# DeltaNet and a quick-GELU feed-forward on one core: the chunk inverses built from blocks of 8, with the joins on TensorE

## The chip, the core and the metric

The kernel runs on one core of a Trainium2 chip. The metric is device time in microseconds of one execution of the whole program. Engines are TensorE (PE, with its weight loads PEld), VectorE (DVE), ScalarE (ACT), GpSimd (POOL) and SyncE (SP, which mostly issues DMA transfers).

## What is computed

A delta-rule attention over 4 batches, 8 heads, 768 steps and head size 48 is followed by a feed-forward of 3072 tokens, 384 to 2048 to 384.

```python
k_n = k / (np.linalg.norm(k, axis=-1, keepdims=True) + 1e-06)
for t in range(S):
    y[:, :, t] = np.einsum('bhd,bhde->bhe', q[:, :, t], state)
    v_old = np.einsum('bhde,bhd->bhe', state, kt)
    state = state + bt[:, :, :, None] * np.einsum('bhd,bhe->bhde', kt, vt - v_old)
...
h = x @ w_in
g = h * (1.0 / (1.0 + np.exp(-1.702 * h)))
return (g @ w_out).astype(np.float32)
```

The weights come in 8-byte floats and are converted on the chip to 4-byte ones.

## The kernel before

The sequence is cut into 6 chunks of C = 128 steps. A unit is a chunk of one batch with all 8 heads (units 0 to 3, first chunk), or, from the second chunk on, half a chunk of 64 steps of two batches (class `Half`). Within a chunk the recurrence becomes a triangular system: with the Gram matrix of the normalized keys (`gram`), the corrected values U solve a unit lower triangular system. Its diagonal blocks of BS = 32 are inverted ahead of time, and the solve runs block by block.

**Inverses.** `diagonal(n)` computes the 32x32 diagonal Gram blocks of a first-chunk unit on TensorE (tile `psD`); VectorE scales them by beta into `XBs`. `invert(c)` puts the 128 blocks of all units on the 128 partitions (VectorE transposes, tiles `NT` and `YB`). For i = 1 to 15 it forms row i of the inverse of both 16-blocks of each 32-block at once: a product into tile `P` and a sum over it (line 308 on). For the first chunk (c = 0) it stops there, scales by beta and transposes back to `XBs`. For later chunks it joins the two 16-blocks to 32 on VectorE as well (lines 318 to 341, ten products and ten sums), scales by beta and sends the result through DRAM to `XBs`. Its input there comes from the Gram matrices through DRAM: `send_blocks` writes blocks to `Nd`, `load_diagonals` reads them into `NT`, and `bL` holds the betas, fetched by 16 transfers issued on POOL.

**The first join.** `merge(pair, ...)` (line 734) joins the 16-blocks of two first-chunk units to 32 on TensorE: VectorE transposes the blocks, a burst of 32x32-tile matmuls forms `psP`, ScalarE evicts it masked by `upper`, a second burst adds into `psZ`, ScalarE copies the corner into `XBs`.

**Solving the first chunk.** Units go in pairs, (0, 1) and (2, 3). `hops` lists eight steps for a pair: `solve` of one 32-block of a unit (`psU`, ScalarE copy into U) beside `below` of the other unit, which subtracts the solved block from the rows under it (accumulated in `psV`, which `gather` has filled with the values; ScalarE copies the next block). `put_out` then forms the outputs `psY` and the state. ScalarE copies them to `xT`, `last` and `ST`, and six transfers move `last` into its place in `xT` (three issued on SP, three on POOL). The scores `psQ` are copied to `M` and masked on POOL (`select`).

**Filling.** `fill(us)` emits pieces of VectorE's background work until their estimated costs reach `us`. The background (line 370) is, in order: conversion of all of w_in and of the first 8 row groups of w_out, then `invert(1)`, then conversion of the other 8 row groups. One conversion piece has five VectorE operations and one on ScalarE (a clamp). `feed()` emits one step (three matmuls of 256 columns) of `hidden`, the first feed-forward product (tile `ph`). `warm(n)` emits n matmuls on constants whose results are not used (tile `ps_warm`). `paced` makes a weight fetch wait for a certain result by a one-element POOL copy.

**Order.** Nearly every operation is issued through wrappers (line 139) that keep an engine's instructions in the order of the program text, so traces show line 139 for them, and so do DMAs issued through `sync` (SP) and `other_queue` (POOL). A few POOL operations, such as the differences of w_out formed in `combined` (shown as line 1118), are placed by the compiler's scheduler.

After the second pair's hops the program emits 25 rounds of `fill(1.0)` and `feed()` together with norms, transposes and Grams of the third chunk's units, the scores of unit 4, half of `both_written` (second feed-forward product, tile `po`), `fill(9.5)`, and from then on slots (`slot(n, share)`). A slot solves a block of unit n and one of unit n + 1, writes outputs, and fills TensorE with feed-forward work from a queue. The inverse of unit 4 is first read at the beginning of slot 3.

## Time and profile before

| what | us |
|---|---|
| median of 3 runs | 692.75 |
| the runs | 686.65, 693.12, 692.75 |
| the profiled execution | 683.09 |
| its span, first to last instruction | 681.4 |
| TensorE busy in the span | 660.4 (97%) |
| VectorE busy | 479.5 (70%) |
| ScalarE busy | 233.6 (34%) |
| GpSimd busy | 269.4 (40%) |
| mean granted clock of TensorE | 0.991 |

The profile is of one execution. A busy TensorE is not TensorE at its peak, since the ends of its matmuls are modelled. A program row such as "TENSOR_TENSOR P<-NT,YB 128x8" names the written tile, the read tiles and partitions x elements. A logical matmul of 4-byte floats has two records, so three matmuls of `hidden` show as x6. A bracket at the end of a row gives the idle time of the engine before it and what ended it.

### The profile page before, as it was taken

What the parts mean: (1) busy time and instruction counts of PE and PEld (TensorE: products, weight loads), DVE (VectorE), ACT (ScalarE), POOL (GpSimd) and SP (SyncE); (2) the same over time, 40 slices, a digit from 0 to 9 for tenths busy, and PEclk for the clock granted to TensorE, in tenths of its full rate; (3) what the DMA queues carried; (4) which work ended last, traced back from release to release, by engine and by line L of the source; (5) the groups of instructions that cost most, each with busy time, mean ns of one, the idle gap of its engine ahead of it and who ended that gap; (6) DMA issues with size and microseconds to landing.
All of it is one profiled execution on the core that took longest, in us unless ns stands there. A gap on an engine that the chain in (4) does not pass through costs nothing.

```text
span 681.4 us, 21731 instructions
## 1 busy us (share of the span) xinstructions
PE 660.4 (97%) x9290; PEld 563.4 (83%) x9290; DVE 479.5 (70%) x890; ACT 233.6 (34%) x571; POOL 269.4 (40%) x282
## 2 busy tenths in 40 slices
PE   9899899799999999999999999999999999999997
PEld 4766678566678998998998988988988988989997
DVE  4889799983788997996997996997976970200000
ACT  2558463632333233333333233233233233322120
POOL 4032844320286634635535526426305205105041
PEclk9799999989999999999999999999999999999999
DMA  9567575263334435335335244244231130100101
GB/s 174 105 165 175 128 218 99 44 155 81 83 74 92 96 63 109 79 67 104 71 67 116 67 90 88 66 86 79 62 78 19 38 75 2 30 2 6 26 0 24
DMA packets 149632, 54.61 MB, mean 80 GB/s; under 512 B 137824, under 2 KB 142656, under 8 KB 149536
## 3 DMA queue, kind: packets, MB, share of 16 engines
q1 hardware_dynamic: 146368, 46.62, 32.7%
q0 software_dynamic: 3168, 6.61, 3.7%
q8 instruction: 73, 1.20, 0.8%
q14 instruction: 23, 0.19, 0.1%
HBM read 38.37 MB, written 13.63 MB: 76 GB/s over the span
## 4 chain that ended last, share of the span: by engine, by line
PE 86%; DVE 6%; ACT 2%; DMA 2%; issue 2%; SPq 1%; DVEq 0%; ACTq 0%
PE po L139 34%; PE ph L139 32%; PE four L139 7%; PE psU L139 3%; PE psR L139 2%; PE psG L139 2%; DVE P L139 2%; DVE w_out L139 2%; PE ps_warm L139 1%; DVE YB L139 1%; DMA TW<-in_q_dram 1%; PE psQ L139 1%; SPq L139 1%; PE psV L139 1%; DVE NT L139 1%
## 5 line engine op out<-in xcount | busy, mean ns | idle before, releaser
L139 PE MATMUL ph<-xT,w_in 128*128 128x256 f32 x1152 | 261.0, 384 | 2.3 <-ACT gT L139 2.0
L139 PEld LDWEIGHTS ph<-xT,w_in 128*128 128x128 f32 x1152 | 215.9, 190 | 33.8 <-ACT gT L139 2.4
L1118 POOL TENSOR_TENSOR gT<-gT 128x512 f32<-128x512 f32 x80 | 103.0, 1298 | 97.9 <-ACT gT L139 66.0
L139 PE MATMUL po<-w_out,gT 128*128 128x192 f32 (+1 forms) x720 | 138.4, 347 | 0.0
L139 DVE TENSOR_TENSOR P<-NT,YB 64x8 f32<-64x8 f32 (+13 forms) x195 | 124.8, 640 | 5.8
L139 PEld LDWEIGHTS po<-w_out,gT 128*128 128x128 f32 x720 | 118.5, 190 | 11.0 <-ACT o L139 0.5
L139 ACT ACTIVATE gT<-ph 128x512 f32<-128x512 f32 x90 | 53.8, 598 | 154.8 <-PE ph L139 154.8
L139 DVE TENSOR_REDUCE YB<-P 64x4 f32<-64x8 f32 (+13 forms) x195 | 78.4, 402 | 6.7
L139 PE MATMUL po<-TW,gT 128*128 128x192 f32 x480 | 81.8, 328 | 0.0
L139 PEld LDWEIGHTS po<-TW,gT 128*128 128x128 f32 x480 | 78.1, 190 | 0.7
L984 POOL TENSOR_SCALAR_AFFINE_SELECT M<-M 64x512 f32<-64x512 f32 x40 | 29.1, 727 | 90.0 <-ACT M L139 88.8
L139 DVE TENSOR_TENSOR o<-o,late 128x192 f32<-128x192 f32 x20 | 6.6, 356 | 68.1 <-ACT late L139 67.9
L139 ACT COPY VU<-psU 32x384 f32<-32x384 f32 x96 | 45.2, 470 | 21.3 <-PE psU L139 14.9
L139 DVE TENSOR_TENSOR VU<-VU,psR 32x384 f32<-32x384 f32 x40 | 22.1, 553 | 36.6 <-PE psR L139 35.9
L400 POOL TENSOR_TENSOR rn<-ssq,half 128x8 f32<-128x8 f32 x12 | 22.3, 1858 | 52.6 <-DVE ssq L139 52.6
L139 DVE TENSOR_TENSOR VU<-VU,four 128x384 f32<-128x384 f32 x19 | 10.4, 548 | 46.1 <-ACT M L139 46.0
L109 POOL DMA_DIRECT2D KN<-in_k_dram x24 | 17.2, 716 | 58.4 <-PE four L139 56.7
L139 ACT COPY o<-po 128x192 f32<-128x192 f32 (+1 forms) x44 | 14.7, 334 | 74.6 <-PE po L139 72.5
L139 PEld LDWEIGHTS psU<-VU,XBs 32*32 32x32 f32 x1536 | 27.4, 105 | 13.5 <-issue 8.5
L139 PE MATMUL psU<-VU,XBs 32*32 32x48 f32 x1536 | 32.6, 203 | 0.3 <-ACT VU L139 0.2
L139 DVE TENSOR_TENSOR P<-NT 64x512 f32<-64x512 f32 (+7 forms) x45 | 30.5, 679 | 1.1
L139 DVE TENSOR_REDUCE NT<-P 64x32 f32<-64x512 f32 (+9 forms) x45 | 30.0, 668 | 1.5
(167 smaller groups left out, 752.1 us busy)
## 6 DMA issues: line engine op xcount, KB each, us to landing
VU<-in_v_dram SPq DMA_DIRECT2D x40, 96.0 KB, 2.8
out_dram<-o SPq DMA_DIRECT2D x40, 96.0 KB, 2.2
QW<-in_q_dram SPq DMA_DIRECT2D x76, 48.0 KB, 2.2
Kd<-KN SPq DMA_DIRECT2D x56, 64.0 KB, 2.2
late<-Kd SPq DMA_DIRECT2D x14, 256.0 KB, 2.8
KN<-in_k_dram POOLq DMA_DIRECT2D x30, 96.0 KB, 3.1
w_out<-in_moe_w_out_dram SPq DMA_DIRECT2D x7, 384.0 KB, 3.8
NT<-Nd SPq DMA_DIRECT2D x20, 128.0 KB, 2.7
```

The lines of the kernel that those rows point to most:

```text
L109: dma(out=place(dst, n)[rows, :, 0:D], in_=src[b, :, t, :].rearrange("h p d -> p h d"),)
L139: return lambda *a, **kw: tc.keep_in_program_order(op(*a, **kw))
L400: nc.gpsimd.tensor_tensor(rn, ssq, half, op=ALU.pow)
L984: nc.gpsimd.affine_select(out=M, in_=M, compare_op=ALU.is_gt, fill=0.0, base=0, pattern=[[0, H], [1, CH]], channel_multiplier=-1,)
L1118: (engine or nc.gpsimd).tensor_tensor(o, a, b, op=op)
```

## The change

The diff is cut here; "..." marks what is left out.

The first chunk. `diagonal` scales by a beta that is zero outside each row's own eighth and sums over eighths, so `XBs` holds only the 8x8 diagonal blocks. `invert_first` takes the place of `invert(0)`: four 8x8 blocks per partition, seven rounds. `spread` writes the inverses back into block-diagonal 32-blocks. `merge` joins on TensorE in three levels, 8 to 16, 16 to 32 and 32 to 64, for both pairs. In the first pair VectorE does part of the evictions, in the second ScalarE does. `solve` and `below` work on blocks of 64, so a pair has three steps, and a step emits both units.

```diff
+        for hh in range(2):
+            vec.tensor_tensor(
+                split[:, hh], ps[hh].rearrange("p j (g k) -> p j g k", g=NE),
+                bG[:, n * H + hh : (n + 1) * H : 2].broadcast_to([128, NP, NE, E8]), op=ALU.mult,
+            )
+        vec.tensor_reduce(
+            XBs[:, n, :, 0:E8], flat.rearrange("p (h g k) -> p h k g", h=H, g=NE), axis=AX.X, op=ALU.add
+        )
...
+    def invert_first():
...
+        vec.transpose(lanes_N.rearrange("p i k -> p k i"), by_lanes(XBs[:, :, :, 0:E8]))
...
+        for i in range(1, E8):
+            P = wk.tile([128, NE, i, i], F32, tag="P", name="P", bufs=1)
+            tt(
+                P, eighths(lanes_N, i * E8, [[0, i], [1, i]]), eighths(lanes_Y, 0, [[E8, i], [1, i]]),
+                op=ALU.mult,
+            )
+            vec.tensor_reduce(
+                eighths(lanes_Y, i, [[E8, i]]), P, axis=AX.X, op=ALU.add, negate=True
+            )
+        tt(lanes_N, lanes_Y, bI.broadcast_to([128, BS, E8]), op=ALU.mult)
+        vec.transpose(packed.rearrange("p n k -> p k n"), lanes_N.rearrange("p j i -> p i j"))
...
+    def merge(pair, area, banks, first):
...
+        for s in (E8, 2 * E8):
...
+            turn_blocks()
+            for X, o, m in zip(pair, odd, Pm):
+                ps = psum(0, "psP", HS)
+                for h in range(H):
+                    for r in rows:
+                        pe.matmul(
+                            ps[r, h, :], lhsT=X.G[r, h, r], rhs=o[r, h], start=True, stop=True,
+                            skip_group_check=True,
+                        )
...
+            for x, o, t, m in zip(Z, odd, XT, Pm):
+                ps = psum(1, "psZ", HS)
...
+                if first:
+                    vec.tensor_tensor(o, o, split, op=ALU.add)
+                else:
+                    act.copy(o, split)
+                yield
+        turn_blocks()
...
+        for i, X in enumerate(pair):
+            W = wides[X.n] = wide[:, i]
...
+        def solve(self, blk):
+            r = slice(blk * CH, (blk + 1) * CH)
+            psU = bank("psU")
+            for h in range(H):
+                pe.matmul(
+                    psU[r, h, :], lhsT=wides[self.n][r, h, :], rhs=self.V[r, h, :],
+                    start=True, stop=True,
+                )
             act.copy(self.U[r], psU[r])
```

The tiles of `invert_first` and the 64-blocks (`wide`) all lie in `NT`. The order around them is written anew: the Gram matrices come after `invert_first`, most `warm` calls go, and the weights of the later quarters, the values of units 2 and 3 and the first rows of w_out are fetched at other places. The second pair runs inside passes of one `feed()` and `fill(2.2)` each. `load_diagonals` and the 16 transfers of `bL` come after the outputs of unit 3.

```diff
+    for X in pair[:2]:
+        X.solve(0)
+    pair[1].gather()
+    next(scored[2])
+    fill(1.5)
+    for X in pair[:2]:
+        X.below()
+    next(scored[3])
+    fill(1.5)
+    paced(pair[0].US[CH : CH + 1, 0:1], 2, 1)
+    for X in pair[:2]:
+        X.solve(1)
...
     put_out(pair[0])
     fill(2.0)
     put_out(pair[1])
+    scaling = roots_second(areas)
+    next(scaling)
+    merging = merge(pair[2:], area, ((ps_seq, "seq"), (ps_seq, "seq")), False)
+    fetch_in(2, js=(2,))
+    for b in range(HB, B):
+        load_values(b, sync)
+    for j in range(KC):
+        fetch_in(3, js=(j,))
+    next(merging), next(merging)
...
+    for X in pair[2:]:
+        X.gather()
...
+    def pass_(us=2.2):
+        feed()
+        fill(us)
...
+    pair[3].select()
+    fetch_out(0, other_queue)
+    fetch_out(1, other_queue)
+    fetch_out(2, other_queue)
+    load_queries(B, other_queue)
...
+    turn(B + 2)
+    put_out(pair[3])
+    pass_()
+    gram(B + 2)
+    turn(B + 3)
+    pass_()
+    Nds.append(send_blocks(B + 2))
+    gram(B + 3)
+    load_diagonals(Nds + [send_blocks(B + 3)])
+    done.add("diagonals")
     for at in range(B):
         for u in range(2):
             for half_ in range(2):
...
```

The second chunk. `invert(1)` no longer joins the 16-blocks. `merge_halves` does it on TensorE at the beginning of slots 3 and 5, for two units each: two VectorE transposes, two bursts `psP` with a ScalarE eviction, two bursts `psZ` with a VectorE addition into `XBs`.

```diff
-        for j, Q in ((0, 2), (2, 2), (4, 4), (8, 4), (12, 4)) if c > 0 else ():
+        for j, Q in ((0, 2), (2, 2), (4, 4), (8, 4), (12, 4)) if c > 1 else ():
...
+    def merge_halves(ns):
...
+        for n, x, m in zip(ns, Z, Pm):
+            ps = one_bank("psP")[:, 0 : H * HS].rearrange("p (h k) -> p h k", h=H)
+            for h in range(H):
+                for k, r in enumerate(rows):
+                    pe.matmul(
+                        ps[r, h, :], lhsT=grams[n][r, h, rows[k % 2]], rhs=x[r, h, HS:],
+                        start=True, stop=True, skip_group_check=True,
+                    )
+            act.activation(m, ps, ACT.Copy, scale=minus)
+            yield
...
+            vec.tensor_tensor(x[:, :, HS:], x[:, :, HS:], ps, op=ALU.add)
...
+    joins = {B - 1: (B, B + 1), B + 1: (B + HB, B + HB + 1)}
     for n in range(B - 1, len(units)):
+        if n in joins:
+            run(merge_halves(joins[n]))
         slot(n, 10.5 if n < B + HB else 19.5)
```

## The prediction

> **What bounds the kernel now.** I read the page first, then busy time by windows, then each engine's timeline up to 160 us.
>
> ```profile
> PE   9899899799999999999999999999999999999997
> DVE  4889799983788997996997996997976970200000
> ...
> PE 86%; DVE 6%; ACT 2%; DMA 2%; issue 2%; SPq 1%; DVEq 0%; ACTq 0%
> ```
>
> ```profile
> 100.00:120.00 20.00, 18.80 (x114) 16.07 (x110) 18.73 (x45) 7.75 (x24) 8.44 (x10) 1.00 0.49 100
> 120.00:140.00 20.00, 15.32 (x120) 12.38 (x121) 19.03 (x40) 13.32 (x43) 7.59 (x6) 0.92 0.34 78
> 140.00:160.00 20.00, 20.00 (x156) 12.66 (x155) 14.14 (x30) 5.56 (x11) 1.74 (x3) 0.99 0.47 106
> 160.00:180.00 20.00, 20.00 (x324) 12.50 (x326) 8.78 (x24) 4.90 (x13) 3.22 (x5) 1.00 0.43 99
> ```
>
> After the span come engine columns PE, PEld, DVE, ACT, POOL, then clock and DMA. From 140 us on TensorE has no gap until the last 81 us (76.8 busy there). What follows 143 us is a wall of fixed work. So the change is worth what it shifts the wall's start, less what it puts into the wall. Before it, VectorE is full (18.7 and 19.0 of 20):
>
> ```profile
> 21.68 2.06 DVE L139 STREAM_TRANSPOSE NT<-XBs 128x1024 f32<-128x1024 f32 x1
> ...
> 103.06 1.22 DVE L139 TENSOR_TENSOR NT<-NT,bL 128x1024 f32<-128x1024 f32 x1
> ...
> 116.23 0.39 DVE L139 COPY NT<-YB 128x256 f32<-128x256 f32 x1
> ...
> 133.09 1.17 DVE L139 TENSOR_TENSOR NT<-YB,bL 128x1024 f32<-128x1024 f32 x1
> ...
> 154.57 0.56 DVE L139 SCALAR_TENSOR_TENSOR w_out<-raw,w_out 128x384 f32<-128x384 f32 x1
> ```
>
> The first inversion takes 21.68 to 38.17, the second 103.06 to 134.18, and the last weight conversion ends at 155.05. On TensorE the wall and the first use of the second inverse are:
>
> ```profile
> 136.84 1.73 PE L139 MATMUL psQ<-QS,kT 48*64 48x112 f32 x32 [3.59 <-ACT QS L139]
> ...
> 143.25 10.59 PE L139 MATMUL po<-w_out,gT 128*128 128x384 f32 x32
> 153.76 0.87 PE L139 MATMUL psU<-VU,XBs 32*32 32x48 f32 x32
> ```
>
> **First chunk.** Gone: 16.5 us of VectorE. New: seven rounds of product and sum on 4i² elements. The old rounds have 2n², so I read across by size: 0.17, 0.18, 0.20, 0.23, 0.27, 0.31, 0.37 = 1.73, twice, plus 14 gaps of 0.04: 4.0. Two transposes of 256 elements at a quarter of 2.06 (0.52; the contiguous 128x256 row, 0.42, is the other end) and a product of 0.4 make 5.5. The start moves from 21.7 to 22.5 (a 0.42 sum per unit; three hide in VectorE's waits for psD, 0.4 to 0.95 each). With one spread (0.4) unit 0's blocks stand at 28.4, against 38.17.
>
> TensorE has four Gram products (7.2 us in the rows of psG, which lie at half clock) and unit 0's scores and turn (2.0) before the first join, from 21.5 on, so the join begins near 30.7, 2 us after its blocks. Each join level is two bursts (psP, psZ) per unit at 0.73, an eviction at 0.37 or 0.3, and 0.77 of VectorE transposes; its chain is 3 to 4 us, so the levels end at 34.8, 37.8 and 41.8. Today one level and eight hops run from 38.7 to 64.7; solve, below, solve are left of the hops. ScalarE then sets the pace: from 37 to the copy of unit 1's output it has evictions 1.5, corner copies 1.5, scores 2.5, six copies of U and V at 0.47 (2.8), squares 1.9, three clamps at 0.94 (2.8), unit 0's copies 1.15 and an estimated 1.3 of gaps: 52.5. That copy started at 67.43, so the first pair is 15 us earlier.
>
> Second pair: its values are now issued on SP behind that copy: three transfers 2.6, four weight transfers 2.4, then 4.5 to land, so gather cannot run before 61.5 and the hidden layer starts at 62.9 (it was 77.2). Nine passes hold 28 us of TensorE: 9 x 1.33 hidden, two join levels 4.6, scores 1.2, solves and below 2.4, turns and Grams 3.2, outputs 3.4 and 1.2 of gaps, to 90.9. Unit 3's copy comes at 92, against 102.96: the gain shrinks to 11 us.
>
> **Second inversion.** The joins taken out are the rows from 116.23 to 133.09 without the 3.2 us of other work between: 13.6 us. But its inputs move. The blocks' way through DRAM and 16 loads of bL now stand behind unit 3's output:
>
> ```profile
> 71.93 9.31 POOL L139 DMA_DIRECT2D bL<-in_beta_dram  x16
> ```
>
> Queued on POOL behind xT (1.5) they are issued from 93.5 to 102.8 and landed near 105.5. After 90.9 two passes, two Grams and a turn (4.7) bring TensorE to 95.7; the last Gram is evicted at 96.5, and the block transfers took 9.5 us from there (84.3 to 93.8): 106. VectorE itself could start at 101.5. From 28.4 it has 51.4 of conversions (pieces of 4.25, 2.98 and 2.35 by their five rows), 6.4 of spreads and first-pair joins, 2.3 of second-pair transposes and 4.4 of norms, 64.5 in all, plus waits: 5.5 within the first joins and 3.1 for weights whose fetches the change moves behind unit 1's copy (third and fourth quarter) and behind unit 3's mask (first output rows). Queued behind the waiting product on VectorE are the norms of later units; their ScalarE scalings wait for those, and TensorE's hidden layer for ScalarE. So the inversion starts at 106.2 (3.1 later than now), runs 16.7 (31.1 less 13.6 and 0.8 of other work that falls outside) and ends at 122.9, 11.3 earlier. The conversions left take 20.9 as now, to 143.8.
>
> **Wall.** TensorE from 95.7: 21 feeds at 1.33 (28), turns and Grams 2.6, scores 1.7, stalls behind those scalings an estimated 4 (5.9 in today's rows of waits): the po run starts at 132 and ends at 142.5. The new join of the second chunk stands here. Its transposes queue on VectorE behind the conversions: 143.8 + 0.8, psZ twice 1.4, and psU starts at 146.1, 7.7 earlier. The other join, two slots later, has no cover: four bursts 2.7 to 3.3, I take 3.0. Sum: 7.7 - 3.0 = **4.7 us gained**. Its lower bound is four bursts at 0.66 with every eviction hidden (2.6), its upper one adds a stall per pair of bursts like the "issue" gaps of 1.0 to 1.5 that today's bursts show (5); I stay near the lower, as only some of today's bursts have one.
>
> Edits at nothing: four small mask sums on VectorE lie in its 2.98 us wait for the first squares; YB's fill (2.2) moves on POOL behind weight issues into its 12.8 idle; the second chunk's keys are issued on SP after values and weights instead of before, land near 42.5 and are read at about 48. If that cover went, each costs its own length at the start of the chain.
>
> **A rule against it.** The change drops most warming matmuls: 50 records, 13.08 us busy, ran between 28 and 65, at clock 1.00.
>
> ```profile
> 18.00:20.00 2.00, 0.51 (x65) 0.40 (x64) 1.28 (x2) 1.15 (x2) 0.00 (x0) 1.00 0.00 0
> 22.00:24.00 2.00, 2.00 (x22) 2.00 (x20) 1.90 (x2) 0.80 (x2) 0.00 (x0) 0.50 0.23 43
> ```
>
> Here 1.5 us of idleness after small tiles was followed by half clock. [...] By the row, rival C below.
>
> **Rivals.**
> A. VectorE stays the bound: blocks and bL land by 101.5. For it: VectorE is over 90% busy up to there, and my 14 us behind the hand-off is a sum of queue waits. Against it: 9.31 us of bL issue is in the trace. Then TensorE alone sets the wall: po from 128.5 (stalls 0.5), to 139, psP and psZ of both units 1.4 each, psU at 142: 11.8 - 3.0 = 8.8 gained.
> B. Slower: bL gets stuck. POOL's unpinned differences of w_out (four, 1.0 to 1.65) already stand in its queue waiting up to 3.9 us for VectorE, ahead of xT. Should those of the last early pieces come before bL, bL starts after about 105, lands at 118.2, 12 later than forecast; VectorE is then behind everything: psU at 158.1, 4.3 later than now, plus 3.0: 7.3 lost. It decides from an inversion start of 110.9 on; beyond 117.8 it is over 1%. Against it: they appear behind the pinned loads in today's order.
> C. Half clock between 31 and 62. A Gram took 1.80 there against 1.16 for the same 16 records of psQ at full clock, a factor of 1.55. On about 13 us of full-size matmuls that is 7 us, half under ScalarE: 3.5 later at each hand-off, leaving about 1 gained.
> That the change does not do what it says is excluded for VectorE, ScalarE and TensorE: their wrappers keep program order.
>
> **Numbers.** The profiled execution took 683.09 us, 1.7 outside its span of 681.4; the forecast for it is 678.4 (span 676.7). The median of 692.75 lies 9.66 above; taking the same difference off it gives 688.0. About 1% (6.9 us) is what a measurement here can tell from nothing. Forecast 0.50, its own range 1 to 9 us gained: 0.15 beyond 1%, 0.35 within. A 0.25, faster. B 0.18, slower. C 0.07, within. So faster 0.40, same 0.42, slower 0.18. The range runs from A with 4 us less in the first pair's chain and the joins at their low bound (13.2, so 679) to B without its last us (699); the runs of the kernel themselves scatter over 6.5 us.
>
> **What would show it.** Right: unit 0's blocks at 28 to 29; unit 1's "last" copy near 52 and unit 3's near 92; an idle VectorE of some 4 us ending with a DMA before the product NT,bL at 106; conversions ending near 144; psU at 146; two join bursts of 64-record groups in the wall, 3 us each. Wrong: a product NT,bL that waits for nothing (A) or starts after 111 (B); clock rows of 0.5 between 31 and 62 (C); unit 1's copy later than 58, which would take the whole gain.

## The result and the profile after

| what | us |
|---|---|
| changed kernel, median of 4 runs | 727.04 (724.21 to 736.45) |
| kernel before in the same comparison, median of 4 runs | 690.0 (686.65 to 693.12) |
| ratio, with its 95% interval | 1.0524 (1.0431 to 1.0617) |
| the changed kernel's profiled execution, its span | 736.45, 734.7 |
| unit 1's `last` copy: before, predicted, after | 67.43, 52.5, 78.44 |
| unit 3's `last` copy: before, predicted, after | 102.96, 92, 135.53 |
| product NT,bL: before, predicted, after | 103.06, 106.2, 153.16 |
| last conversion ends: before, predicted, after | 155.05, 143.8, 190.88 |
| first psU of the wall: before, predicted, after | 153.76, 146.1, 194.33 |
| first long run of the next hidden layer: before, after | 200.10, 253.45 |

The change costs 5% where 0.7% of gain was forecast. From the last row on, the two kernels run at the same pace: the difference there, 53.35, is the difference of the two spans, 53.3. So the whole loss lies ahead of it. The profiled execution of the changed kernel lies more than 1.5% above the fastest of its four runs and is therefore left out of comparisons (the median of the other three is 725.09), and that of the kernel before, 683.09, lies below its median, so marks of the two profiles are up to 53 us apart where the medians are 35 apart.

The page of the changed kernel: busy tenths of TensorE and VectorE in 40 slices of 18.4 us, the clock granted to TensorE, and the chain of waits.

```profile
PE   8869879997897999999999999999999999999997
DVE  6543654779335789979879799699795993110000
...
PEclk9655777999897999999999999999999999999999
...
PE 87%; DVE 5%; issue 4%; DMA 2%; SPq 1%; ACT 1%; DVEq 0%; ACTq 0%
```

The same clock row of the kernel before, in slices of 17.0 us:

```profile
PEclk9799999989999999999999999999999999999999
```

VectorE is now idle early, where it was full. But TensorE does not run at full clock either: the clock row has 6, 5, 5 in slices 2 to 4 and 7 in the next three, where the kernel before has 7 and then 9s, and "issue", time in which an engine waits for nothing that the profile shows, went from 2% to 4% of the chain. The windows give both in numbers (columns as in the prediction: span, then busy time of PE, PEld, DVE, ACT, POOL, then clock and DMA).

```profile
20.00:40.00 20.00, 16.56 (x421) 14.99 (x425) 11.00 (x32) 7.31 (x16) 1.40 (x3) 0.57 0.68 133
40.00:60.00 20.00, 16.27 (x453) 13.93 (x446) 6.76 (x16) 5.15 (x13) 1.27 (x2) 0.50 0.24 47
60.00:80.00 20.00, 19.39 (x287) 16.62 (x286) 11.38 (x16) 9.92 (x25) 0.90 (x3) 0.57 0.12 28
100.00:120.00 20.00, 19.00 (x235) 15.33 (x235) 8.54 (x16) 7.65 (x19) 4.18 (x7) 0.57 0.10 32
180.00:200.00 20.00, 17.90 (x325) 11.68 (x324) 10.73 (x25) 4.32 (x10) 0.69 (x1) 0.83 0.44 94
```

Half clock stands in nearly all of 20 to 80 us, while TensorE shows 16 to 19 of 20 us busy and VectorE 7 to 11. The first pair on TensorE's timeline:

```profile
34.14 1.90 PE L147 MATMUL psP<-XBs,gT 32*32 32x16 f32 x128
35.87 1.12 PE L147 MATMUL psZ<-P 32*32 32x16 f32 x69
39.47 0.98 PE L147 MATMUL psZ<-P 32*32 32x16 f32 x58 [2.48 <-issue]
...
43.48 0.98 PE L147 MATMUL psP<-XBs,gT 32*32 32x16 f32 x58 [2.10 <-issue]
...
46.96 1.03 PE L147 MATMUL psZ<-P 32*32 32x16 f32 x60 [1.58 <-issue]
47.93 3.62 PE L147 MATMUL psP<-XBs,gT 32*64 32x32 f32 x64
...
58.27 3.64 PE L147 MATMUL psU<-VU,NT 64*64 64x48 f32 x32
```

Three things are to be seen. After each stretch of some 128 records the engine stops for 1.58 to 2.48 us with nothing to wait for. 128 records of psP take 1.90 us at half clock, where the prediction had 1.46. And one psU of both units, 32 records of 64x64, takes 3.64 us at half clock, where the prediction had 0.8 (2.4 for three such steps). VectorE, by contrast, does what was forecast, only later:

```profile
23.26 0.67 DVE L147 STREAM_TRANSPOSE NT<-XBs 128x256 f32<-128x256 f32 x1
...
151.05 0.55 DVE L147 TENSOR_REDUCE ssq<-ksq 128x8 f32<-128x384 f32 x1 [3.06 <-ACT ksq L147]
...
153.16 2.23 DVE L147 TENSOR_TENSOR NT<-NT,bL 128x1024 f32<-128x1024 f32 x1
...
169.27 1.18 DVE L147 TENSOR_TENSOR NT<-YB,bL 128x1024 f32<-128x1024 f32 x1
...
190.32 0.56 DVE L147 SCALAR_TENSOR_TENSOR w_out<-raw,w_out 128x384 f32<-128x384 f32 x1
```

The second inversion runs 17.3 us (16.7 predicted), and the conversions left take 20.4 behind it (20.9 predicted). The join of the second chunk in the wall then reads:

```profile
189.42 1.31 PE L147 MATMUL psP<-XBs,G 32*32 32x16 f32 x128
191.38 0.90 PE L147 MATMUL psZ<-P 32*32 32x16 f32 x81 [0.65 <-DVE P L147]
193.72 0.82 PE L147 MATMUL psZ<-P 32*32 32x16 f32 x45 [1.45 <-issue]
...
194.39 1.46 PE L147 MATMUL psU<-VU,XBs 32*32 32x48 f32 x31
195.79 6.30 PE L147 MATMUL po<-w_out,gT 128*128 128x384 f32 x12
```

A pause of 1.45 splits the burst, and the 12 records of po after it take 6.30 us where the kernel before takes 4.14. From that psU to the long run of the hidden layer there are 59.1 us; before there were 46.3.

### The profile page after: what moved, and what is told of

Same layout as the page of the kernel before. It is cut to its first block, busy times and chain, and to the rows that moved or that the text cites. A ratio compares the mean times of both kernels' runs of the same rounds, so it can differ in the third digit from the quotient of the medians.

```text
span 734.7 us, 23320 instructions
## 1 busy us (share of the span) xinstructions
PE 697.9 (95%) x10072; PEld 599.5 (82%) x10072; DVE 467.3 (64%) x890; ACT 235.2 (32%) x579; POOL 267.5 (36%) x282
## 3 DMA queue, kind: packets, MB, share of 16 engines
q8 instruction: 79, 1.29, 0.7%
## 4 chain that ended last, share of the span: by engine, by line
PE 87%; DVE 5%; issue 4%; DMA 2%; SPq 1%; ACT 1%; DVEq 0%; ACTq 0%
PE ph L147 32%; PE po L147 31%; PE four L147 7%; PE psU L147 4%; PE psR L147 2%; PE psZ L147 2%; PE psG L147 2%; PE psP L147 2%; PE psV L147 2%; DVE w_out L147 1%; PE psQ L147 1%; DMA KN<-in_k_dram 1%; PE psT L147 1%; PE psY L147 1%; DVE P L147 1%
## 5 line engine op out<-in xcount | busy, mean ns | idle before, releaser
L147 PE MATMUL ph<-xT,w_in 128*128 128x256 f32 x1152 | 264.5, 387 | 3.2 <-ACT TW L147 1.8
L147 PE MATMUL po<-w_out,gT 128*128 128x192 f32 (+1 forms) x720 | 141.9, 353 | 0.0
L147 DVE TENSOR_TENSOR P<-NT,YB 64x512 f32<-64x512 f32 (+23 forms) x175 | 116.1, 664 | 5.0
L147 DVE TENSOR_REDUCE YB<-P 64x2 f32<-64x2 f32 (+24 forms) x175 | 70.1, 401 | 6.0
L147 ACT COPY VU<-psU 32x384 f32<-32x384 f32 (+1 forms) x88 | 41.4, 471 | 30.1 <-PE psU L147 28.2
L147 DVE TENSOR_TENSOR VU<-VU,four 128x384 f32<-128x384 f32 x19 | 10.4, 549 | 46.0 <-ACT M L147 45.9
L117 POOL DMA_DIRECT2D KN<-in_k_dram x24 | 17.1, 714 | 58.1 <-PE four L147 47.3
L147 DVE TENSOR_TENSOR P<-NT 64x512 f32<-64x512 f32 (+10 forms) x47 | 28.9, 616 | 1.4
L147 DVE TENSOR_REDUCE NT<-P 64x32 f32<-64x512 f32 (+11 forms) x47 | 28.3, 603 | 1.6
L147 ACT COPY xT<-four 128x256 f32<-128x256 f32 (+1 forms) x40 | 13.1, 328 | 45.1 <-PE four L147 45.1
L147 PE MATMUL psZ<-P 32*32 32x16 f32 (+1 forms) x832 | 13.5, 200 | 13.3 <-issue 12.6
```

The costliest lines, as they stand in the source:

```text
L117: dma(out=place(dst, n)[rows, :, 0:D], in_=src[b, :, t, :].rearrange("h p d -> p h d"),)
L147: return lambda *a, **kw: tc.keep_in_program_order(op(*a, **kw))
```

## The experiments

The first four runs ask after the pauses, the clock, and the second chunk's half of the change. Three numbers behind a run are its median and, in brackets, its least and greatest time; the ratio is to the kernel before. Differences to the changed kernel are taken from its 725.09.

**e1_warm**: matmuls on constants put back into the changed kernel (`warm(n)` emits n / 2 matmuls of 512 columns).

```diff
     gram(1)
+    warm(16)
...
             act.copy(m, ps)
+            if first or not ffn:
+                warm(4)
             yield
...
     for X in pair[:2]:
         X.solve(0)
+    warm(4)
```

> The changed kernel with matmuls on constants put back on TensorE: 8 of 512 columns after the second Gram product, 2 after each burst of the first pair's joins and of the second pair's first level, 2 after solve and below. Theory 1 (the lost clock is the cause): the granted clock is 1.00 from about 27 us on, 32 records of psU take 2.0 us instead of 3.6, unit 1's output copy comes near 64 instead of 78, and the whole takes about 700 us, some 27 less than the changed kernel. Theory 2 (TensorE runs out of instructions: every pause called issue in the changed kernel comes 128 matmul records, with their 128 weight loads, after the one before): the pauses of 1.3 to 2.5 us stay where the joins are, since a matmul that has not been delivered cannot fill them; the gain is 12 us at most.

It took 735.95 (729.99 to 740.25), ratio 1.0682 (1.0593 to 1.0772): slower than the changed kernel, where theory 1 had hoped for a gain. In the first pair the matmuls ran at the pace of full clock only from 29 to 39 us (two records on constants 0.61 at 35.11 and 36.31, 1.03 from 39.65 on; the mean clock from 20 to 40 is 0.81). Of the three pauses at the joins one is left, of 1.91 us, so two of them were filled, which theory 2 had excluded; yet unit 1's copy came at 85.31, later than in the changed kernel. These are the windows of this run:

```profile
40.00:60.00 20.00, 19.90 (x437) 11.63 (x437) 6.43 (x16) 2.13 (x6) 0.17 (x1) 0.50 0.29 62
60.00:80.00 20.00, 20.00 (x168) 15.33 (x162) 6.18 (x9) 7.32 (x15) 1.27 (x2) 0.50 0.11 27
```

TensorE is shown busy for 39.9 of these 40 us, some 12 of them on constants (12 times 1.03), and the clock is 0.50 throughout. So idleness that the profile shows is not what holds it down, and this edit does not test what full clock is worth.

**e2_vector_join**: the changed kernel, with the second chunk's join back on VectorE.

```diff
-        if c > 1:
+        if c > 0:
...
-        if n in joins:
-            run(merge_halves(joins[n]))
```

> The changed kernel with the second chunk's blocks joined on VectorE again, as before the change (no join bursts at slots 3 and 5). If the bursts cost what the prediction said (3.0 us each on TensorE, against 13.6 us of VectorE on the way to the inverse), it is 5 to 8 us slower than the changed kernel. If each burst brings pauses and a stretch at half clock, as the changed kernel's rows from 189 to 241 us suggest (59 us from the first psU to the next hidden product, 46 before), the loss and the gain nearly cancel: within 4 us of the changed kernel, and from the first psU to the next hidden product 46 to 47 us.

717.16 (714.84 to 721.15), ratio 1.042 (1.033 to 1.0509). Moving that join to TensorE costs 7.9 us in the changed kernel (725.09 against 717.16), although it takes 14.4 us off the inversion on VectorE. That is neither theory's number, and from the first psU to the next hidden product it took 50.9, not 46 to 47.

**e3_second_only**: the kernel before, with that half of the change alone.

> The kernel before with only the second chunk's part of the change. Its inversion ends 13.6 us earlier (near 120.6 instead of 134.2). If the bursts cost 3.0 us each, the whole is 1 to 4 us faster than the kernel before. If they bring pauses and half clock, some 13 to 16 us in all from 143 to 215 us, it is 8 to 12 us slower.

705.31 (703.01 to 706.78), ratio 1.0241 (1.0176 to 1.0305): some 15 us worse than the kernel before, more than either theory had. The inversion is 14.4 us long instead of 31.2, yet the po run comes only 1.7 us sooner after its start than in the kernel before (151.48 - 112.96 = 38.5 against 143.25 - 103.06 = 40.2). With VectorE relieved, TensorE's own work is most of what is left (from 113 to 152 us it is busy 34.2 of 39); the two joins with their pauses (1.83, 2.39 and 2.17) come on top. The first pair of this run, whose code is that of the kernel before, ran into something else:

```profile
37.98 0.73 PE L139 MATMUL psP<-XBs,gT 32*32 32x16 f32 x64
...
40.31 0.71 PE L139 MATMUL psQ<-TW,kT 48*128 48x128 f32 x7
44.03 0.58 PE L139 MATMUL psQ<-TW,kT 48*128 48x128 f32 x1 [3.02 <-issue]
```

The same place has a pause of 1.00 in the profile of before, and no loss of clock (1.00 from 27.7 to 136.9). Here it is 3.02, from 44 to 60 the matmuls take nearly twice as long (four records on constants 1.89 instead of 1.04), and the product NT,bL comes at 112.96 instead of 103.06. That is not what this run's loss is made of: from unit 3's copy to the end of the span it takes 591.7 us, against 578.4 in the kernel before, 13.2 more. The profiles of e4 and e6 show the long pause as well (2.26, and 2.25 with four matmul records more ahead of it), so the profile of before is the rarer case. In the kernel before the queue that the page lists as "instruction" (q8) has a packet of some 16 KB in flight shortly before TensorE goes on: at 40.25 for the end of the pause at 42.78. In the changed kernel the packets at 36.00, 41.00 and 44.50 belong to the pauses that end at 39.47, 43.48 and 46.96. So I read a pause as the wait for the next block of instructions, 2.5 to 3.5 us after its packet is seen. The page of the changed kernel has 79 such packets with 1.29 MB, 16.3 KB each; TensorE's 10072 matmul records and 10072 weight loads come to 255.0 a packet, and the 9290 and 9290 of the kernel before, whose page has 73, to 254.5. In the changed kernel 128 records with their loads stand between the pauses that end at 39.47 and 43.48, and 127 between that and the one that ends at 46.96. So I take a block as some 256 instructions.

**e4_bursts**: the kernel before, with bursts of extra matmuls of 32x32 ahead of six slots.

```diff
+    sizes = {9: (64, 16), 11: (128, 16), 13: (256, 16), 15: (64, 128), 17: (128, 128), 19: (256, 128)}
     for n in range(B - 1, len(units)):
+        if n in sizes:
+            burst(*sizes[n])
         slot(n, 10.5 if n < B + HB else 19.5)
```

> The kernel before with bursts of extra matmuls on constants ahead of slots 9, 11, 13 (64, 128, 256 matmuls of a 32x32 tile with 16 columns, two records each) and 15, 17, 19 (the same counts with 128 columns). Results of the extra matmuls are not used. Theory 1: no pauses inside a burst; 128, 256 and 512 records of 16 columns take 1.3, 2.6 and 5.3 us (0.0103 each, the rate of the changed kernel's psP rows), and the clock may fall behind the long ones. Theory 2: each further 128 records need about 4 us: the bursts of 256 and 512 records take 4 to 6 and 12 to 14 us, with one pause per 128 records; those of 128 columns have none, as they run no faster than the supply.

The first number of a pair counts matmuls (two records each), the second columns. The rows show the burst of 256 matmuls with 16 columns up to its second pause, and the one with 128 columns:

```profile
393.10 1.83 PE L139 MATMUL ps_burst<-ident 32*32 32x16 f32 x196
397.16 1.91 PE L139 MATMUL ps_burst<-ident 32*32 32x16 f32 x128 [2.23 <-issue]
400.88 1.32 PE L139 MATMUL ps_burst<-ident 32*32 32x16 f32 x84 [1.82 <-issue]
...
569.55 14.18 PE L139 MATMUL ps_burst<-ident 32*32 32x128 f32 x512
```

512 records of 16 columns stop every 128 records and stretch a slot pair from 49.6 to 66.8 us. 512 records with eight times the columns take 14.18 without a pause, less than the 17.2 that the others cost. The bursts of 256 and 512 records of 16 columns took 5.0 and 12.8, as theory 2 had it. 64 matmuls of 16 columns alone took 1.1 to 1.2 us and no pause. It is not the matrix work that costs: about 128 records with their 128 weight loads, 256 instructions, are used up in 1.2 to 1.9 us, and the next block is there after some 4 us (from the end of one pause to the end of the next 3.72 here, 4.01 and 3.48 in the first pair of the changed kernel). After the first pause the clock fell to 0.50 here too, from 397.2 to 410 at least.

**e5_tiles**: the same with 32 matmuls (64 records) of one kind each time.

```diff
+        9: (64, 64, [(0, 0)], 48), 11: (64, 64, [(0, 0), (64, 64)], 48),
+        13: (32, 32, [(0, 0)], 48), 15: (32, 32, four_at, 48),
+        17: (32, 64, [(32, 0), (96, 64)], 32), 19: (128, 128, [(0, 0)], 48),
```

> The kernel before, with 32 extra matmuls (64 records) of one kind ahead of six slots: weights of 64x64 on one tile of the array, 48 columns; the same on two tiles in turn; weights of 32x32 on one tile, 48 columns; the same on four tiles in turn; weights of 32x64 on two tiles in turn, 32 columns; weights of 128x128, 48 columns. The psU of the changed kernel (64x64, one tile, 32 records) took 1.8 to 2.2 us at full clock, 56 to 68 ns a record, where the prediction had some 28. Theory 1 (matmuls on the same tile wait for each other, since the next weights cannot be loaded while the tile is in use): one tile costs 55 ns a record whatever its size, 3.5 us for 64 records, and two or four tiles in turn half of that or less. Rival (the price goes by size): 64x64 costs 3.5 us on one tile and on two, and 32x32 costs 1.8 on one tile and on four.

Five of the six bursts on the timeline (the third has 61 of its 64 records in this row):

```profile
286.04 4.21 PE L139 MATMUL ps_burst<-ident 64*64 64x48 f32 x64
...
342.56 2.07 PE L139 MATMUL ps_burst<-ident 64*64 64x48 f32 x64
...
394.11 2.77 PE L139 MATMUL ps_burst<-ident 32*32 32x48 f32 x61
...
446.35 0.88 PE L139 MATMUL ps_burst<-ident 32*32 32x48 f32 x64
...
550.31 8.78 PE L139 MATMUL ps_burst<-ident 128*128 128x48 f32 x64
```

Sixty-four records of 64x64 take 4.21 us on one tile and 2.07 on two in turn; of 32x32, 2.9 on one and 0.88 on four. Theory 1 holds in its times, except that the size counts as well on one tile; that the loading of the weights is the cause, as it has it, these times do not show. What they show is the price of staying on one tile. In the windows of the last burst the clock falls while TensorE is busy without a gap:

```profile
552.00:554.00 2.00, 2.00 (x20) 2.00 (x20) 1.90 (x4) 0.00 (x0) 1.72 (x2) 1.00 0.03 8
554.00:556.00 2.00, 2.00 (x19) 2.00 (x18) 1.84 (x5) 0.00 (x0) 0.00 (x0) 0.93 0.00 0
556.00:558.00 2.00, 2.00 (x11) 2.00 (x11) 1.83 (x6) 0.00 (x0) 0.00 (x0) 0.50 0.28 62
```

Weights of 128 columns for 48 columns of data: PE and PEld both show 2.00 of 2.00, and some 5.4 us after the start of the burst the clock is halved (a mean of 0.93 in the window from 554 puts the fall at 555.7).

**e6_fill_pause**: the kernel before, with dense work put in ahead of its pause in the first pair.

```diff
     for i in range(HB):
         next(products)
+        if i:
+            warm(8)
         next(scored)
```

> The kernel before, with four matmuls on constants (1.9 us) between the second psP burst of the first pair and the scores after it, where its profile shows a pause of 1.00 us for instructions and where the runs that came out some 10 us longer show 2.26 and 3.02. Theory 2 (a block of 256 instructions is fetched some 2.5 to 3.4 us after it is asked for, and a pause over about 2 us halves the clock for some 16 us): the pause falls below 1.2 us, the clock stays at 1.00 between 42 and 60 us, and all runs lie within 682 to 687, against 683 to 694 for the kernel before, a ratio of 0.99 to 1.00. Rival (the scatter of the kernel before has another cause): the runs scatter as before and the median is 691 to 693, 1 to 2 us up by the added work.

690.96 (682.37 to 695.21), ratio 1.0011 (0.9958 to 1.0063): no change can be told, as the rival had it (691 to 693). The added work took 1.04 us, not 1.9; the packet came at 41.50, and the pause was still 2.25, with the clock at 0.50 after it. As an answer to the theory it is no more than inconclusive: the dose was too small.

**e7_spread_join**: e3 with the same join bursts one at a time between products of the feed-forward.

```diff
-        if n in joins:
-            run(merge_halves(joins[n]))
...
+    for i in range(HF // 2):
+        ahead_of(both, 2)
...
+        next(joining)
...
+        next(joining[0], None)
```

The last line stands at the end of `spend`, which a slot calls four times.

> The kernel before with the second chunk's part of the change alone, as in e3_second_only (705.31), but its bursts of 64 records stand one at a time between products of the feed-forward: for units 4 and 5 after every second pair of steps of the po run, for units 6 and 7 at the four points of slot 3 at which it takes feed-forward work. The same instructions in another order. Theory 2 (instruction supply): no pause over 0.5 us and a clock of 1.00 from 150 to 225 us; 9 to 13 us of the 57.4 between the first psU and the feed-forward product after it go, and the time is 692 to 697. Rival (the join costs by its instructions, its evictions and its 64-record bursts themselves, wherever they stand): 702 to 706.

701.33 (698.83 to 704.2), ratio 1.0181 (1.0122 to 1.0239), between both numbers. The first four bursts ran without a pause at 0.73 each and full clock. Of the other four, the last stood directly ahead of a psU of 64 records, and 1.74 of pause followed, with the four records of po after it at 2.38 instead of 1.56. From the first psU to the hidden layer's run it took 52.7, against 57.4 in e3 and 46.3 before. From unit 3's copy to the end of the span it takes 586.3, 7.8 more than the kernel before, where e3 took 13.2 more. So a part of e3's loss is the crowding, but the join still costs its own bursts, eight at 0.65, on an engine that was the bound there.

**e8_long_warm**: e1 with 12 matmuls on constants in a row after the first level.

```diff
-                    warm(4)
+                    warm(24 if first and s == E8 and x is Z[1] else 4)
```

> The changed kernel with the matmuls on constants of e1_warm (735.95) and, after the last psZ burst of the first level of the first pair, 12 of them in a row (5.1 us at half clock) in place of 2. In e1 the clock stayed at 0.50 from 40 to 80 us with TensorE shown busy throughout, half of it on constants. Theory 3 (a half clock, once there, ends only after some 3 to 7 us of dense work, and dense work every second microsecond then holds the full clock): 1.00 from about 52 us on, the first psU in 2.2 us or less, unit 1's copy 5 to 12 us earlier than in e1 less the 4 us added, total 722 to 732. Rival (small tiles pull the clock down whatever stands between them): 0.50 again within 8 us of the long stretch, total 738 to 742.

736.56 (734.77 to 739.72), ratio 1.0696 (1.0635 to 1.0756). The long stretch, 4.88 us, brought the clock back to 1.00 from 46 to 50, and a psP burst of 64 to 0.73. By 54 it was 0.50 again, with TensorE shown busy 4.00 of 4.00 in each window up to 70 and psU at 3.64. The rival's clock; neither theory's time.

Three runs then took two suspected sizes out of the changed kernel.

**e9_even**, **e10_half** and **e11_both** (the two edits together):

```diff
+    def solves(Xs, blk):
+        at = [(X, slice(k * CH, (k + 1) * CH), bank("psU")) for X in Xs for k in [(blk + X.n) % 2]]
+        for h in range(H):
+            for X, r, psU in at:
...
-                for h in range(H):
+                for h in range(0, H, 2):
                     for r in rows:
                         pe.matmul(
-                            ps[r, h, :], lhsT=X.G[r, h, r], rhs=o[r, h], start=True, stop=True,
+                            ps[r, h : h + 2, :], lhsT=X.G[r, h, r], rhs=o[r, h : h + 2], start=True, stop=True,
```

> The changed kernel with the two units of a pair solved head by head in turn, and the second unit's two 64-blocks taken in the opposite order, so that neighbouring matmuls of psU and psV lie on different 64x64 tiles of the array (in e5_tiles 29 ns a record on two tiles in turn, 62 on one). Units 1 and 3 are thereby solved in the wrong order. Number and shapes of all instructions stay. Theory 1 (same tile) predicts psU of both units in about 1 us at full clock and 1.9 at half, against 1.8 to 2.2 and 3.6; over six steps that is 1 to 1.8 us each, 7 to 11 us, total 716 to 721. Rival (the stretch around them is set by ScalarE and the clock, not by these bursts): psU shorter, total 724 to 729.

> The changed kernel with each join matmul of the first chunk (psP and psZ, all three levels, both pairs) taking two heads' columns at once with the first head's matrices: half the matmuls, each twice as wide, the same evictions. Odd heads are joined with the wrong matrices. It takes out 640 of the 1280 join records and as many weight loads, 1280 instructions. Theory 2 (instruction supply: 256 instructions for each 3.5 to 4.5 us of a dense burst, and pauses that pull the clock down): at most one pause over 1.5 us between 34 and 48 us instead of three, the clock at 1.00 in part of 30 to 78, unit 1's `last` copy 6 to 14 us earlier, total 704 to 715. Rival (the time goes by columns and by the chain of evictions): pauses gone, clock as before, total 720 to 727.

> The edits of e9_even and e10_half together (the wrong order for units 1 and 3, the wrong matrices for odd heads). If the two prices are independent, the gains add: 696 to 710. If the half clock is the common carrier of both, the second edit gives more or less than alone. Rival (neither matters, the chain of evictions does): above 718.

The next table sets them beside the two kernels. The marks are from the timelines of the profiled executions, whose own time stands beside them.

| kernel | unit 1's copy | unit 3's copy | NT,bL | profiled | median | ratio (interval) |
|---|---|---|---|---|---|---|
| before | 67.43 | 102.96 | 103.06 | 683.09 | 690.0 | |
| changed | 78.44 | 135.53 | 153.16 | 736.45 | 725.09 | 1.0524 (1.0431 to 1.0617) |
| e9_even | 72.58 | 118.15 | 137.44 | 718.36 | 723.66 | 1.0493 (1.0428 to 1.0558) |
| e10_half | 68.62 | 110.86 | 129.51 | 712.13 | 712.96 | 1.032 (1.0265 to 1.0374) |
| e11_both | 62.91 | 104.21 | 126.17 | 708.55 | 709.16 | 1.0253 (1.0193 to 1.0314) |

In e10 no "issue" pause is left between 25 and 130 us. Theory 2's time is met (704 to 715), but hardly its clock: it stays 0.50 from 22.6 to 67.0, although no join has a pause any more. Six hundred and forty records fewer are worth 12.1 us. In e9 psU of both units takes 1.94 at half clock instead of 3.64, and the copies come 6 and 17 us earlier. In the two profiled executions that gain reaches the end (from unit 3's copy on, both take 599 us), but of the medians only 1.4 us is left, about what the rival had; beside e10 it is 3.8. The ranges of e9 and of the changed kernel overlap (718.36 to 725.74 and from 724.21 on), so alone it is not told from nothing.

**e12_filled**: e6 with twice the dense work, and some before the second pair's psZ bursts.

```diff
+            warm(16)
...
+                warm(8)
                 next(merging)
```

> The kernel before with eight matmuls on constants (1.8 us at full clock) where e6_fill_pause had four, and four more (0.9 us) before each psZ burst of the second pair, where the profiles show pauses of 1.13 to 1.97 us. In e6 the pause after the first addition still was 2.25 us, as the fetched block of instructions came 0.5 to 1.25 us later than in the profile of before, and the clock fell. Theory 2: the first pause is now about 1.2 us and the clock stays at 1.00 from 42 to 60 us; median 684 to 688, no run above 691, so at least as fast as the kernel before (689.39) and up to 0.8% faster. Rival (the added instructions only shift the block boundary, and pauses and clock scatter as before): 690 to 694.

685.75 (682.88 to 692.59, 12 runs) beside 689.56 (679.36 to 695.97, 17 runs) for the kernel before; ratio 0.9991 (0.9949 to 1.0033). The windows of e6 and of e12 where the pause was:

```profile
42.00:46.00 4.00, 1.75 (x10) 1.06 (x10) 2.48 (x5) 0.62 (x2) 3.66 (x1) 0.73 0.10 21
46.00:50.00 4.00, 4.00 (x76) 2.26 (x75) 3.70 (x7) 1.13 (x3) 0.31 (x1) 0.50 0.09 22
```

```profile
42.00:46.00 4.00, 3.45 (x82) 1.91 (x81) 2.52 (x4) 0.65 (x2) 3.84 (x1) 1.00 0.14 33
46.00:50.00 4.00, 4.00 (x99) 2.74 (x98) 3.90 (x9) 1.96 (x5) 0.65 (x2) 1.00 0.61 139
```

The pause is 0.55, the clock stays at 1.00 up to 98 us and beyond, and NT,bL comes at 103.23. The median is in theory 2's range (684 to 688), and eleven of twelve runs lie below 690.2. That is the mechanism, shown in one profile. That the kernel is faster than before is not shown: the interval takes in 1, and one run, at 692.59, is above the bound named.

**e13_rest** and **e14_keys_first**: e11 with the second chunk's join back on VectorE, and this with the keys of units 8 and 9 fetched ahead of bL.

```diff
+    load(8, ((KN, k),), sync)
+    load(9, ((KN, k),), other_queue)
     for at in range(B):
         for u in range(2):
             for half_ in range(2):
...
-    load(8, ((KN, k),), sync)
-    load(9, ((KN, k),), other_queue)
```

> The edits of e11_both (half the join matmuls, the two units of a pair on different tiles; units 1 and 3 solved in the wrong order, odd heads joined with the wrong matrices) and of e2_vector_join (the second chunk's join back on VectorE). It asks whether the three prices found make up the loss of the changed kernel. e11 took 709.16, and the second chunk's join cost 9.9 inside the changed kernel (727.04 against 717.16). If the prices are independent: 697 to 702, and what is left over the kernel before (689.56) is the later start of the second inversion (22 us behind unit 3's copy in e11, where before it was at it). If the second chunk's join is hidden now, as TensorE waits more: 706 to 711.

> e13_rest (with the same parts computed wrongly) and the key transfers of units 8 and 9 issued ahead of the 16 transfers of bL on POOL and not behind them. In e11 VectorE waited 8.19 us ahead of the product NT,bL for a norm of keys whose transfer POOL issued only after bL's 9.04 us of issue. Theory (what was left is POOL's queue): that wait falls below 2 us, bL lands 4.2 us later, the product starts 3 to 5 us earlier, and the time falls by 2 to 5 us against e13. Rival (bL itself, landing 4.2 us later, takes the place of the keys): the product no earlier than in e13, and the same time within 1.5 us.

e13: 695.02 (692.42 to 699.57), ratio 1.0062 (1.0038 to 1.0087), below both ranges: the second chunk's join costs 14.1 here (709.16 against 695.02), where it cost some 15 on the kernel before and 7.9 in the changed kernel. By the stretch from unit 3's copy to the end of the span it is 10.0 here, 13.2 there and 12.1 in the changed kernel, so that its price depends on the first chunk isn't shown. e14: 693.98 (692.39 to 695.92), ratio 1.0053 (1.0022 to 1.0084). In the two profiles the product NT,bL moves from 128.49 to 123.96, and the wait ahead of it from 9.52 to 5.25, not below 2; the medians differ by 1.04, which is within the rival's 1.5, and the intervals overlap. POOL's queue is a part of the delay; that it is worth anything at the end isn't shown.

## Why the prediction was wrong

**The step that failed** is the price of TensorE's bursts of small matmuls: "two bursts (psP, psZ) per unit at 0.73", "solves and below 2.4", and "four bursts 2.7 to 3.3, I take 3.0". The rows were right; 0.73 for 64 records is what an undisturbed burst takes (e7). But in the kernel before these bursts stood between dense matmuls on constants, and the change puts them one behind the other. Three things follow that the prediction gave no price or too small a one; half clock lengthens all three.

- Supply of instructions. The prediction saw the "issue" gaps of 1.0 to 1.5 us, used them as the upper bound for the second join alone, and gave the first chunk none. They are, as the packets and counts of e3 have it, the wait for a block of some 256 instructions. Half the first chunk's join records are worth 12.1 us in the changed kernel (e10, in which pauses and the bursts' own time go together).
- One tile. The prediction does not say from which row it took 0.8 a step; it fits the psU row that it shows, 32 records of 32x32 in 0.87. The 64x64 matmuls of both units lie on one tile: 2.06 us at full clock (psV of the second pair), 3.64 at half, in place of 0.8. Worth 3.8 beside e10 (e11); alone, 1.4 that is not told from nothing (e9).
- The second join in the wall. Forecast net: 7.7 gained less 3.0. Measured: 7.9 lost in the changed kernel, 14.1 with the first chunk's sizes mended, some 15 on the kernel before. e7 gives back 4 of it by spreading alone.

Taking them in this order the median goes 725.1, 713.0, 709.2, 695.0, beside 690.3 for the kernel before. What is left is 0.6% (0.4 to 0.9).

**Point by point.**

- First blocks: predicted at 28.4, they were spread by about 29.5. Right: the rounds cost what the rule by size gave (0.16 to 0.36 a step), the transposes 0.67 instead of 0.52.
- Join begins 30.7: it began at 34.14. The prediction had half clock for the Gram matrices alone; the scores ran at it as well (15 records of psQ 2.38, against 1.16 for 16 in the kernel before), and two turns at 1.11 stood ahead of the join.
- Levels end at 34.8, 37.8 and 41.8: they ended at 40.5, 48.0 and 56.3. Wrong, by pauses of 6.2 in sum and by half clock.
- Unit 1's copy at 52.5, and a copy later than 58 as what would take the whole gain: it came at 78.44, 11 later than in the profile of before. The profiles of e3, e4, e5 and e7, whose first pair is the kernel before's, have it at 74.03 to 76.18; beside those it is some 3 us late, and the larger loss arises in the second pair: 57.1 us from this copy to unit 3's, against 34.6 to 39.2 there, with four pauses of 1.28 to 2.40.
- The second pair's wait for its values, 10.4 us from that copy to the hidden layer: 12.1. Right (its parts, 2.6, 2.4 and 4.5 behind 52.5, make 62.0, where the prediction has 61.5). Its nine passes, 29 us from the hidden layer to unit 3's copy: 45.0 in the changed kernel, 29.4 in e11 (74.85 to 104.21), which has the bursts at about the predicted size. So the plan of the passes was right, and its terms for bursts were not.
- The inversion starts 14 behind the hand-off, unit 3's copy, with VectorE idle before it until a transfer lands: 17.6 behind, with 3.06 idle. The queue is the predicted one, POOL behind bL (issued 138.17 to 147.24). But what came last was not bL: a norm of unit 9's keys, whose transfer is queued behind bL, stands ahead of the product on VectorE.
- Inversion 16.7 and conversions 20.9: 17.3 and 20.4. Right.
- VectorE as what sets the wall: e3 speaks against it. With 17 us less of inversion the po run came 1.7 us sooner. Part of the gain hoped for was never there, as rival A's "TensorE alone sets the wall" had it.

**The rivals.** A had the bound but not its time. B did not come: bL was issued right behind the xT transfers and did not get stuck. C, half clock, came: from 22.7 to 77.3 us, from 84.1 to 91.0, from 101.2 to 118.3, and behind both joins of the wall (193.4 to 200.2 and 230.9 to 241.2). The first of these does not come from the joins' pauses: it begins ahead of the first join, at the place where the kernel before has it too (20.9 to 27.7), and it goes on here as it does in e10 (22.6 to 67.0), whose joins have no pause. C was given 0.07 and 3.5 us a hand-off, as it took 13 us of full-size matmuls as its base and no pauses.

**The clock.** The prediction's sum prices half clock for the Gram matrices alone; the clock was 0.50 from 22.7 to 77.3. The longest wait of TensorE in that stretch was 2.48 us, and the clock was 0.50 ahead of it and behind it; e1 and e8 hold it at 0.50 with TensorE shown busy (39.9 of 40 us, and 4.00 of 4.00 in each window from 54 to 70), and e5 loses it inside an unbroken burst (1.00, 0.93, 0.50, busy 2.00 of 2.00). So here busy in the profile is not what keeps the clock. The times of its switches do show a step: read in windows of 0.1 us, the switches in the profiles of the kernel before and of the changed kernel lie whole multiples of 3.41 us apart (6.8 in the kernel before at 20.9 to 27.7; 54.6, 6.8 and 17.1 in the changed kernel at 22.7 to 77.3, 84.1 to 91.0 and 101.2 to 118.3), and switches worked out from the means of 4 us windows fit the same step (17.0 in e6 at 43.8 to 60.9, 44.4 in e10 at 22.6 to 67.0). The row that the prediction showed, 1.5 us of slack after small tiles and then 0.50, pointed to rival C. On supply, size and count agree (16.3 KB a packet, a pause every 128 records and loads), and in bursts of 16 columns the wait shows: 1.58 to 2.48 us each in the first pair.

**What stays open.** How much of the first pair is half clock by itself: no run held full clock through it, and e13, at 695, still has 0.50 from 20 to 60 us. It is open too what in a burst takes the clock down while the profile shows TensorE busy, and why the profiled executions of e3, e4 and e6 had a long pause at 42 us and that of before a short one: in e6 the packet came later (41.50 instead of 40.25) while transfers were denser (a DMA share of 1.05 from 38 to 42 us, against 0.84), but that these hold it up was not tried.

## What to carry to other kernels

Price a burst of small matmuls by its instructions as well as by its columns: here some 256 of them, weight loads included, were good for one block (255 a packet), and a burst that used them up in 1 to 2 us then stopped for 1.3 to 3.0. Interleave such bursts with wide matmuls that have to be done anyway (4 us gained in e7; constants put between them in e1 cost more than they saved), turn between tiles of the array (2.07 us against 4.21 for 64 records of 64x64 in e5), and read the granted clock behind each "issue" pause, since the half clock that follows may cost more than the pause (17.0 us of it behind 2.25 in e6). And before work moves from a full engine to another, look whether the other is the bound where the work lands.

## What was not expected of the hardware

- The clock halved under an unbroken run of matmuls whose weights outweigh their data: 1.00, 0.93, 0.50 in three windows of 2 us with TensorE busy 2.00 in each (e5, 128x128 weights and 48 columns), likewise within 4 us for 64x64 on one tile (e5, burst from 286.04, mean clock 0.87 from 288 to 290 and then 0.50). A burst of 128 columns on 32x32 tiles, 14.18 us long, did not do it: the 64 records of psU behind it took 0.86 us, as at full clock (e4).
- Once halved it stayed so for 6.8 us where dense work followed (e5, 555.7 to 562.6), for 17.0 or 44.4 in mixed work (e6, 43.8 to 60.9; e10, 22.6 to 67.0), each a whole multiple of 3.41, and dense work of 4.88 us brought it back for 6.8 us only (e8, 45.9 to 52.7).
- One record of the same 32x32 shape took 14 ns in turn over four tiles and 45 on one (e5: 0.88 and 2.9 us for 64).
